# Seven-product steps: groups of products kept five places from their piece, copies first

## Chip, cores and metric

One core of a Trainium2 chip. The metric is the device time of one execution in microseconds; the program runs on one core, so its time is that core's.

## The reference, cut to what matters

```
X = rfft(x)                      # x: 2 x 3008 x 256
Y = shrink(X @ w + b)            # complex product, soft threshold
x = irfft(Y)                     # 6016 x 256
h = x @ w_in                     # first part, d_ff = 2048
x = (h * clip(h + 3, 0, 6) / 6) @ w_out
g = x @ w_gate                   # second part, d_ff = 1536
out = (silu(g) * (x @ w_val)) @ w_out2
```

All in float32. The kernel reaches float32 accuracy with three matmuls of a rounded type per product: each operand is split in a high half (a rounding copy, ScalarE) and a low half (the difference, VectorE).

## The kernel before, in words

The Fourier stage comes first, then the first part on the 6016 tokens, then the second. Tokens go in six pairs of two blocks, five pairs with 512 columns a block and a last one with 448. The first two pairs of the first part are computed plainly, unit by unit (`unit`, L552; its side work is in `beside`, L763). The other four pairs take **seven-product steps** (`quad1`, L875): a step has two blocks of tokens and two column groups of w_in, and gets their four products from seven (a Strassen scheme) instead of eight. The stage has 4 pairs x 8 steps = 32 steps. `quad` (L969) does the same for the second part in 72 steps.

A step of `quad1` runs so. `product` (L815) is three matmuls (L821 to L823). Products 1, 7 and 2 open the PSUM banks P, T and Q; ScalarE copies 1 and 7 out (`keep`, L868: c1, c7). VectorE adds c1 to Q (`add`, L863): v0, the first of four results. Product 6 is accumulated on P behind product 1 and copied (cu), 4 on T, whose sum with cu is g0; 5 on P, whose sum with c7 is g1; 3 on P again, which is the fourth result, read from P itself. Each result goes through `gate` (L855, ScalarE) and `times` (L859, VectorE) and then, by `give` (L845), through `split` (cast L517 on ScalarE, low half L130 on VectorE) into a *piece*. For each piece `give` puts two *groups* (three matmuls each, L125 to L127, into the accumulators of the output product) on the list `pending`. `fill` (L840) takes the first group from the list, if there is one; a step calls it at eight **places**. The multiply and split of the fourth result are left to the next step (`end_of`, L871), which does them ahead of its first product. A step so has 21 matmuls of products and 24 of groups.

The engines take their instructions in the order in which the program lists them, each engine for itself (the schedule is manual), and wait on semaphores between them. So an instruction that waits holds everything listed behind it on its engine.

`todo.send()` (L833) runs the next step of side work; it stands in four spots of a step. `beside1` (L932) says what it is: **operand steps** for the next pair (`operands`, L674: four differences and seven splits of the pair's tokens, `raw`, one instruction each, 18 in all) and **side steps** (`side`, L750), one step each of the chain that turns weights into the form of the seven products: for the second part, per block of weights, three word steps (VectorE and a scaling on ScalarE, L168 to L186), a step with the weight sums (L594, VectorE) and their cast into a ring slot (L632, ScalarE), a step with the low half, and one with the last low half and the store to memory (L639). The chain has twelve such blocks. What of it isn't done in the first part is done by two `side()` calls in each step of `quad`.

The ring has four slots of weights (`ring`, L589); `fetch` (L742) loads a step's weights two steps ahead on SP's queue, and the casts of the side chain take slots of the same ring. In steps 0 and 1 of a pair the tokens of the next pair come from the inverse transform (`post_raw`, L728: small matmuls L481 from a table `ct` that `load_ct`, L468, loads on SP's queue). At the end of a block, `finish1` (L507) copies an accumulator out and stores it on SP's queue. In `quad`, `share` (L976) runs the groups of the step before, and in the first step what is left on `pending`.

Of the kernel before, what the change touches and what calls it, by code (L numbers as in the profile page):

```python
# [83 lines left out]
def fourier_moe_kernel(ctx: ExitStack, tc: tile.TileContext, x, lin, bias, w1, w2, fwd1, inv2, fwd2,  # L84
# [342 lines left out]
    P = [lambda n=n: pre_conv(n) for n in range(NB * NT)]  # L427
# [246 lines left out]
    def operands(s, p, load=None):  # L674

        n = halves[p]
        todo = []

        def b(k, t):
            return raw[s][:, k, t * n : t * n + n]  # L680

        B[s] = {}
        T = {}

        def sub(i, x, y):
            T[i] = cv.tile([128, BLK], F32, tag="T", name=f"T{i}", bufs=3)
            nc.vector.tensor_tensor(out=T[i][:, :n], in0=x(), in1=y(), op=ALU.subtract)

        def hi(m, x):
# [12 lines left out]
        def r(k, j):  # L702
            return lambda: b(k, j)

        of = {1: r(0, 0), 7: t(3), 5: t(1), 6: t(2), 4: t(4), 2: r(1, 0), 3: r(1, 1)}
        subs = {5: (1, r(0, 1), r(0, 0)), 6: (2, r(1, 1), t(1)), 4: (4, r(1, 0), t(2)), 7: (3, r(1, 1), r(0, 1))}
        if load:
            todo += [load, lambda: None]
        for m, x in of.items():
            if m in subs:  # L710
                todo.append(lambda m=m: sub(*subs[m]))
            todo.append(lambda m=m, x=x: hi(m, x))
            todo.append(lambda m=m, x=x: lo(m, x))
        return todo

    def room_for(s):
        raw[s] = cv.tile([128, 2, 2 * BLK], F32, tag="raw", name=f"raw{s}", bufs=1)
# [45 lines left out]
    def beside(n):  # L763
        if not conv1.done():
            conv1.step()
        elif n < last - 1:
            side(1 + (n % 3 == 0))
        f = n - last
        if f in (0, 4, 8):
            load_ct(blocks[2 * S0 + f // 4])  # L770
        if f in (2, 3, 6, 7):
            if f == 2:
                begin_ops(f)
            post_raw(S0, f // 4, f % 4 - 2, bank)
        if f in (4, 5):
            next(ops)()
        if f >= 8:
            for _ in range(2 + f % 2):
                next(ops, lambda: None)()
        if f in (9, 13):  # L780
            fetch((f - 9) // 4)
# [28 lines left out]
    def acc_of(t, e):  # L810
        return (lambda shape, name: one_bank(spot[0], shape, name)) if t and e else acc_bank
# [25 lines left out]
    pending = []  # L837
    tail = []

    def fill(k=1):  # L840
        for _ in range(k):
            if pending:
                pending.pop(0)()

    def give(s, j, t, i, g):  # L845
        k, f = blocks[2 * s + t], 2 * j + i
        hi, lo = split(ghring(), glring(), g, halves[s])
        order = [(jj, ii) for jj in range(KF1 // 2) for ii in ((0, 1) if t == 0 else (1, 0))]
        at = order.index((j, i))
        for e in range(2):  # L850
            pending.append(lambda e=e: out1(k, f, e, hi, lo, at == 0, at == len(order) - 1, acc_of(t, e), "r"))

    def gate(x, n):
        r = xs_p.tile([128, BLK], F32, tag="r", name="r", bufs=3)
# [13 lines left out]
        nc.scalar.copy(c, x[:, :n])  # L868
        return c

    def end_of(q):  # L871
        if tail:
            tail.pop()()

    def quad1(q):  # L875


        s, j = quads1[q]
        n = halves[s]
        fetch(q + ASK)  # L880
        P, T, Q = bank_p(q), one_bank(spot[0] + 3, [128, BLK], "Tb"), bank_q([128, BLK], "Q")
        product = multiply(B[s], q, n)
        end_of(q)
        product(P, 1, start=True)
        c1 = keep(P, n)
        product(T, 7, start=True)
        c7 = keep(T, n)
        product(Q, 2, start=True)
        todo.send()
        v0 = add(Q, c1, n)  # L890
        r = gate(v0, n)
        fill()
        product(P, 6)
        cu = keep(P, n)
        fill()
        times(r, v0, n)
        product(T, 4)
        todo.send()
        g0 = add(T, cu, n)
        give(s, j, 0, 0, r)  # L900
        r = gate(g0, n)
        fill()
        if j < 2 and s + 1 < len(pairs):
            post_raw(s + 1, j, 0, bank_q)
        times(r, g0, n)
        fill()
        product(P, 5)
        g1 = add(P, c7, n)
        give(s, j, 0, 1, r)
        r = gate(g1, n)  # L910
        fill(2)
        if j < 2 and s + 1 < len(pairs):
            post_raw(s + 1, j, 1, bank_q)
            if j == 0:
                load_ct(blocks[2 * s + 3])
        todo.send()
        times(r, g1, n)
        fill()
        product(P, 3)
        give(s, j, 1, 1, r)  # L920
        fill()
        rv = gate(P, n)
        todo.send()
        slot.pop(q)

        def v1():
            times(rv, P, n)
            give(s, j, 1, 0, rv)

        tail.append(v1)  # L930

    def beside1(s):  # L932
        nxt = s + 1
        if nxt < len(pairs):
            o = operands(nxt, nxt)
            gap = 8
        else:
            o = operands(len(pairs), 0, from_dram(len(pairs), 0))
            gap = 2
        o = iter(o)  # L940
        for i in range(4 * (KF1 // 2)):
            if i < gap:
                if i % 3 != 1:
                    yield side
                else:
                    yield lambda: None
            elif i % 3 == 2:
                yield side
            else:
                def two(k=1 + (i % 2)):  # L950
                    for _ in range(k):
                        next(o, lambda: None)()
                yield two
        assert next(o, None) is None

    for q, (s, j) in enumerate(quads1):
        if q == 0:
            lower(units[-1])
            pending += outp(units[-2]) + outp(units[-1])
        if j == 0:  # L960
            todo.steps = beside1(s)
        quad1(q)
        if j == KF1 // 2 - 1 and s + 2 < len(pairs):
            load_ct(blocks[2 * s + 4])
# [4 lines left out]
    def quad(q):  # L969
# [5 lines left out]

        def share(t, e):  # L976
            if before is None:
                fill(2)
# [45 lines left out]
        end_of(q)  # L1024
        product(P, 1, start=True)
        c1 = keep(P, n)
        product(T, 7, start=True)
        c7 = keep(T, n)
        product(Q, 2, start=True)
        v0 = add(Q, c1, n)  # L1030
        if before is not None:
# [5 lines left out]
        side()  # L1037
        todo.send()
        share(0, 0)
        product(T, 4)  # L1040
# [11 lines left out]
        side()  # L1052
        todo.send()
        share(1, 0)

        last = q == len(quads2) - 1
# [59 lines left out]
```

## Time and profile before

| | us |
|---|---|
| median of 3 runs | 1284.1 (1282.96 to 1285.37) |
| the profiled execution | 1285.6 |
| its span, first to last instruction | 1283.8 |
| first seven-product step of the first part to the last | 345.5 to 734.5 |
| steps of the second part | from 734.5 |

The profile's busy shares of the span are PE 96%, DVE 70%, ACT 58%, POOL 1%; the granted clock of TensorE is 0.996 on average. In the profile PE is TensorE's matmuls, PEld its weight loads, DVE VectorE, ACT ScalarE, SP the engine that issues most DMAs; a q behind the name (SPq) is the engine's sequencer. A row of a timeline has the start, the duration, engine, line, operation, the tile written and those read, shapes, and in brackets the idle time of the engine just before it with what ended it. A row of stretches has its bounds, its length, the busy time (and instructions) of PE, PEld, DVE, ACT and POOL, the granted clock, and what the DMA engines did. Matmuls overlap: each lasts longer than the distance to the next.

### The profile page before, as it was taken

The numbers are of one execution on the slowest core, as the hardware profiler recorded it, in microseconds if no ns is written. First come the engines' busy times: TensorE is split into PE (matmuls) and PEld (weight loads), VectorE is DVE, ScalarE is ACT, GpSimd is POOL, SyncE is SP. The second block draws the span as 40 slices with busy tenths as digits, with TensorE's granted clock in tenths as the row PEclk, the third lists the DMA queues.
The fourth block names the chain that finished last, engine by engine and source line by source line (L and its number), as shares of the span: only waits on it lengthen the run. The fifth ranks groups of instructions, "written<-read, shape, count | busy, mean of one in ns | idle before, by whom it ended". The sixth has DMA issues, their size and how long they took to land.

```text
span 1283.8 us, 16138 instructions
## 1 busy us (share of the span) xinstructions
PE 1234.4 (96%) x5818; PEld 1006.0 (78%) x5818; DVE 902.3 (70%) x1606; ACT 742.6 (58%) x1348; POOL 11.1 (1%) x19
## 2 busy tenths in 40 slices
PE   8899999999999999999998999999999999999998
PEld 3699888888876686676776777788888888888897
DVE  3577686775677777777777778677677677666665
ACT  3355565555666666666666655666566556555554
POOL 3000000000000000000000000000000000000000
PEclk9999999999999999999999999999999999999999
DMA  7876222342334352261353366564454544644551
GB/s 283 314 230 196 82 75 100 127 151 73 145 117 148 123 201 101 103 216 71 140 188 120 139 216 227 185 222 174 176 191 170 206 166 161 233 148 151 214 183 68
DMA packets 54688, 209.62 MB, mean 163 GB/s; under 512 B 5376, under 2 KB 19040, under 8 KB 42976
## 3 DMA queue, kind: packets, MB, share of 16 engines
q1 hardware_dynamic: 47360, 199.43, 44.4%
q10 hardware_dynamic: 7056, 8.50, 1.8%
q8 instruction: 45, 0.74, 0.2%
q0 software_dynamic: 192, 0.66, 0.1%
q14 instruction: 35, 0.29, 0.1%
HBM read 162.17 MB, written 46.40 MB: 162 GB/s over the span
## 4 chain that ended last, share of the span: by engine, by line
PE 72%; DVE 13%; ACT 10%; issue 3%; DMA 2%; SPq 0%; ACTq 0%; DVEq 0%
PE acc L127 8%; PE acc L125 8%; PE acc L126 8%; PE P L821 6%; PE P L823 5%; PE P L822 5%; DVE r L859 4%; ACT gated L517 3%; ACT r L855 3%; PE Tb L823 3%; PE Tb L821 3%; PE Tb L822 3%; PE p L481 3%; PE ph L125 2%; PE ph L127 2%
## 5 line engine op out<-in xcount | busy, mean ns | idle before, releaser
L868 ACT COPY hold<-P 128x512 f32<-128x512 f32 (+1 forms) x208 | 119.1, 572 | 61.0 <-PE P L823 60.9
L130 DVE TENSOR_TENSOR gated<-s,gated 128x512 fp32r<-128x512 f32 (+1 forms) x144 | 97.4, 676 | 50.1 <-ACT gated L1003 49.4
L130 DVE TENSOR_TENSOR gated<-r,gated 128x512 fp32r<-128x512 f32 (+1 forms) x128 | 86.1, 673 | 54.3 <-ACT gated L517 51.7
L517 ACT CAST gated<-r 128x512 fp32r<-128x512 f32 (+1 forms) x128 | 77.6, 606 | 72.3 <-DVE r L859 72.3
L127 PE MATMUL acc<-gated,slot 128*128 128x512 f32 (+1 forms) x288 | 111.1, 386 | 0.0
L125 PE MATMUL acc<-gated,slot 128*128 128x512 f32 (+1 forms) x288 | 111.1, 386 | 0.0
L125 PE MATMUL acc<-gated,w_o 128*128 128x512 f32 (+1 forms) x256 | 102.4, 400 | 8.9 <-ACT gated L517 8.6
L126 PE MATMUL acc<-gated,slot 128*128 128x512 f32 (+1 forms) x288 | 111.0, 385 | 0.0
L127 PE MATMUL acc<-gated,w_o 128*128 128x512 f32 (+1 forms) x256 | 103.0, 402 | 4.8 <-DVE gated L130 4.7
L126 PE MATMUL acc<-gated,w_o 128*128 128x512 f32 (+1 forms) x256 | 98.4, 384 | 0.0
L863 DVE TENSOR_TENSOR hold<-Tb,hold 128x512 f32<-128x512 f32 (+1 forms) x104 | 70.3, 676 | 39.0 <-PE Tb L823 36.7
L1043 ACT ACTIVATE s<-hold 128x512 f32<-128x512 f32 (+1 forms) x72 | 44.8, 623 | 90.2 <-DVE hold L863 90.2
L855 ACT ACTIVATE r<-hold,three 128x512 f32<-128x512 f32 (+1 forms) x96 | 68.2, 710 | 49.6 <-DVE hold L863 42.4
L821 PE MATMUL P<-xo,slot 128*128 128x512 f32 x208 | 83.9, 403 | 11.7 <-ACT hold L868 10.7
L863 DVE TENSOR_TENSOR hold<-P,hold 128x512 f32<-128x512 f32 (+1 forms) x104 | 70.3, 676 | 34.9 <-PE P L823 34.7
L863 DVE TENSOR_TENSOR hold<-Q,hold 128x512 f32<-128x512 f32 (+1 forms) x104 | 70.3, 676 | 33.8 <-PE Q L823 25.0
L1003 ACT CAST gated<-s 128x512 fp32r<-128x512 f32 (+1 forms) x144 | 88.0, 611 | 10.2 <-DVE s L1060 8.9
L859 DVE SCALAR_TENSOR_TENSOR r<-r,hold 128x512 f32<-128x512 f32 (+1 forms) x96 | 64.7, 674 | 32.2 <-ACT r L855 31.3
L822 PE MATMUL P<-xo,slot 128*128 128x512 f32 x208 | 81.2, 390 | 0.0
L823 PE MATMUL P<-xo,slot 128*128 128x512 f32 x208 | 81.2, 390 | 0.0
L130 DVE TENSOR_TENSOR gs<-r,gs 128x512 fp32r<-128x512 f32 x64 | 44.1, 689 | 40.9 <-ACT gs L517 40.2
L127 PEld LDWEIGHTS acc<-gated,w_o 128*128 128x128 f32 x256 | 48.0, 187 | 29.9 <-DVE gated L130 22.2
(168 smaller groups left out, 3087.5 us busy)
## 6 DMA issues: line engine op xcount, KB each, us to landing
slot<-Wd SPq DMA_DIRECT2D x72, 1152.0 KB, 5.1
slot<-Sd SPq DMA_DIRECT2D x32, 896.0 KB, 5.1
st<-in_w SPq DMA_DIRECT2D x68, 256.0 KB, 4.2
Wd<-slot SPq DMA_DIRECT2D x12, 1152.0 KB, 5.1
Sd<-slot SPq DMA_DIRECT2D x8, 896.0 KB, 3.5
z<-Bd SPq DMA_DIRECT2D x12, 512.0 KB, 5.5
Cd<-cs ACTq DMA_DIRECT2D x12, 512.0 KB, 3.6
Xd<-x SPq DMA_DIRECT2D x20, 256.0 KB, 2.0
```

Of the source, the lines that this page charges most:

```text
L125: nc.tensor.matmul(o, wl, xh, start=start, stop=False)
L126: nc.tensor.matmul(o, wh, xh, start=False, stop=False)
L127: nc.tensor.matmul(o, wh, xl, start=False, stop=stop)
L130: nc.vector.tensor_tensor(out=o, in0=full, in1=hi.bitcast(F32), op=ALU.subtract)
L517: nc.scalar.copy(hi[:, :n], g[:, :n])
L821: nc.tensor.matmul(o, wl, x[m][:, 0, :n], start=start, stop=False, skip_group_check=not start)
L822: nc.tensor.matmul(o, wh, x[m][:, 1, :n], start=False, stop=False, skip_group_check=not start)
L823: nc.tensor.matmul(o, wh, x[m][:, 0, :n], start=False, stop=True, skip_group_check=not start)
L855: nc.scalar.activation(r[:, :n], x[:, :n], AF.Relu, bias=three)
L859: nc.vector.scalar_tensor_tensor(out=r[:, :n], in0=r[:, :n], scalar=6.0, in1=x[:, :n], op0=ALU.min, op1=ALU.mult)
L863: nc.vector.tensor_tensor(out=h, in0=x[:, :n], in1=c, op=ALU.add)
L868: nc.scalar.copy(c, x[:, :n])
```

## The change

`fill` takes a group only where at least five places have gone by since its piece was given; `drain` takes them without that rule, for the first step of the second part. In `quad1` and `quad` the copy of product 1 comes ahead of the old step's fourth result, whose multiply comes behind that copy and whose split behind the v0 add. The sends stand behind the copy of product 1, behind the copy of product 6 (ahead of the multiply of v0), behind the multiply of g0 and behind the multiply of g1. An operand step now has a copy on ScalarE and, on VectorE, a difference or the low half of an earlier copy: 11 steps. Side steps take three of the four sends in the first three steps of a pair and one send a step later: 14 for a pair, 56 in all, where there were 50 (13, 13, 13, 11). The second half of the inverse transform comes in step 2. In `quad` there is one send, and the two side steps stand together.

```
@@ -674,7 +674,6 @@
     def operands(s, p, load=None):
 
         n = halves[p]
-        todo = []
 
         def b(k, t):
             return raw[s][:, k, t * n : t * n + n]
@@ -704,14 +703,18 @@
 
         of = {1: r(0, 0), 7: t(3), 5: t(1), 6: t(2), 4: t(4), 2: r(1, 0), 3: r(1, 1)}
         subs = {5: (1, r(0, 1), r(0, 0)), 6: (2, r(1, 1), t(1)), 4: (4, r(1, 0), t(2)), 7: (3, r(1, 1), r(0, 1))}
-        if load:
-            todo += [load, lambda: None]
-        for m, x in of.items():
-            if m in subs:
-                todo.append(lambda m=m: sub(*subs[m]))
-            todo.append(lambda m=m, x=x: hi(m, x))
-            todo.append(lambda m=m, x=x: lo(m, x))
-        return todo
+        order = ((1, "sub", 7), (7, "lo", 1), (2, "sub", 5), (5, "lo", 7), (0, "sub", 6), (6, "lo", 2), (0, "sub", 4),
+                 (4, "lo", 6), (3, "lo", 5), (0, "lo", 4), (0, "lo", 3))
+
+        def step(h, what, m):
+            if h:
+                hi(h, of[h])
+            if what == "sub":
+                sub(*subs[m])
+            else:
+                lo(m, of[m])
+
+        return ([load] if load else []) + [lambda c=c: step(*c) for c in order]
 
     def room_for(s):
         raw[s] = cv.tile([128, 2, 2 * BLK], F32, tag="raw", name=f"raw{s}", bufs=1)
@@ -772,10 +775,8 @@
             if f == 2:
                 begin_ops(f)
             post_raw(S0, f // 4, f % 4 - 2, bank)
-        if f in (4, 5):
-            next(ops)()
         if f >= 8:
-            for _ in range(2 + f % 2):
+            for _ in range(2 - f % 2):
                 next(ops, lambda: None)()
         if f in (9, 13):
             fetch((f - 9) // 4)
@@ -837,10 +838,19 @@
     pending = []
     tail = []
 
+    LAG = 4
+    clock = [0]
+
     def fill(k=1):
         for _ in range(k):
+            clock[0] += 1
+            if pending and clock[0] - pending[0][0] > LAG:
+                pending.pop(0)[1]()
+
+    def drain(k):
+        for _ in range(k):
             if pending:
-                pending.pop(0)()
+                pending.pop(0)[1]()
 
     def give(s, j, t, i, g):
         k, f = blocks[2 * s + t], 2 * j + i
@@ -848,7 +858,7 @@
         order = [(jj, ii) for jj in range(KF1 // 2) for ii in ((0, 1) if t == 0 else (1, 0))]
         at = order.index((j, i))
         for e in range(2):
-            pending.append(lambda e=e: out1(k, f, e, hi, lo, at == 0, at == len(order) - 1, acc_of(t, e), "r"))
+            pending.append((clock[0], lambda e=e: out1(k, f, e, hi, lo, at == 0, at == len(order) - 1, acc_of(t, e), "r")))
 
     def gate(x, n):
         r = xs_p.tile([128, BLK], F32, tag="r", name="r", bufs=3)
@@ -868,9 +878,8 @@
         nc.scalar.copy(c, x[:, :n])
         return c
 
-    def end_of(q):
-        if tail:
-            tail.pop()()
+    def end_of():
+        return tail.pop()() if tail else lambda: None
 
     def quad1(q):
 
@@ -880,83 +889,78 @@
         fetch(q + ASK)
         P, T, Q = bank_p(q), one_bank(spot[0] + 3, [128, BLK], "Tb"), bank_q([128, BLK], "Q")
         product = multiply(B[s], q, n)
-        end_of(q)
         product(P, 1, start=True)
         c1 = keep(P, n)
+        end = end_of()
+        todo.send()
         product(T, 7, start=True)
         c7 = keep(T, n)
         product(Q, 2, start=True)
-        todo.send()
         v0 = add(Q, c1, n)
+        end()
         r = gate(v0, n)
         fill()
         product(P, 6)
         cu = keep(P, n)
+        todo.send()
+        times(r, v0, n)
         fill()
-        times(r, v0, n)
         product(T, 4)
-        todo.send()
         g0 = add(T, cu, n)
         give(s, j, 0, 0, r)
         r = gate(g0, n)
         fill()
-        if j < 2 and s + 1 < len(pairs):
-            post_raw(s + 1, j, 0, bank_q)
+        if j in (0, 2) and s + 1 < len(pairs):
+            post_raw(s + 1, j // 2, 0, bank_q)
         times(r, g0, n)
+        todo.send()
         fill()
         product(P, 5)
         g1 = add(P, c7, n)
         give(s, j, 0, 1, r)
         r = gate(g1, n)
         fill(2)
-        if j < 2 and s + 1 < len(pairs):
-            post_raw(s + 1, j, 1, bank_q)
+        if j in (0, 2) and s + 1 < len(pairs):
+            post_raw(s + 1, j // 2, 1, bank_q)
             if j == 0:
                 load_ct(blocks[2 * s + 3])
+        times(r, g1, n)
         todo.send()
-        times(r, g1, n)
         fill()
         product(P, 3)
         give(s, j, 1, 1, r)
+        rv = gate(P, n)
         fill()
-        rv = gate(P, n)
-        todo.send()
         slot.pop(q)
 
         def v1():
             times(rv, P, n)
-            give(s, j, 1, 0, rv)
+            return lambda: give(s, j, 1, 0, rv)
 
         tail.append(v1)
 
     def beside1(s):
-        nxt = s + 1
-        if nxt < len(pairs):
-            o = operands(nxt, nxt)
-            gap = 8
+        s += 1
+        if s < len(pairs):
+            o, do = iter(operands(s, s)), []
         else:
-            o = operands(len(pairs), 0, from_dram(len(pairs), 0))
-            gap = 2
-        o = iter(o)
+            o = iter(operands(s, 0, from_dram(s, 0)))
+            do = [next(o)]
         for i in range(4 * (KF1 // 2)):
-            if i < gap:
-                if i % 3 != 1:
-                    yield side
-                else:
-                    yield lambda: None
-            elif i % 3 == 2:
-                yield side
-            else:
-                def two(k=1 + (i % 2)):
-                    for _ in range(k):
-                        next(o, lambda: None)()
-                yield two
+            if i < 12:
+                do += [side] * (i % 4 != 3)
+            elif i % 2 == 0 or i == 31:
+                do.append(next(o))
+            elif i % 4 == 1:
+                do.append(side)
+            yield lambda: [g() for g in do]
+            do = []
         assert next(o, None) is None
 
     for q, (s, j) in enumerate(quads1):
         if q == 0:
             lower(units[-1])
-            pending += outp(units[-2]) + outp(units[-1])
+            pending += [(-LAG, g) for u in units[-2:] for g in outp(u)]
         if j == 0:
             todo.steps = beside1(s)
         quad1(q)
@@ -975,7 +979,7 @@
 
         def share(t, e):
             if before is None:
-                fill(2)
+                drain(2)
                 return
             (pb, fb), w, g = before
             if (pb, t, e) not in acc:
@@ -1021,20 +1025,20 @@
         fetch(F0 + q + ASK)
         P, T, Q = bank_p(F0 + q), one_bank(spot[0] + 3, [128, BLK], "Tb"), bank_q([128, BLK], "Q")
         product = multiply(B[len(pairs) + p], F0 + q, n)
-        end_of(q)
         product(P, 1, start=True)
         c1 = keep(P, n)
+        end = end_of()
         product(T, 7, start=True)
         c7 = keep(T, n)
         product(Q, 2, start=True)
         v0 = add(Q, c1, n)
+        end()
         if before is not None:
             (pb, fb), w, g = before
             hi = split_hi(g[1], pb)
             g[1] = (hi, split_lo(g[1], hi, pb))
         product(P, 6)
         cu = keep(P, n)
-        side()
         todo.send()
         share(0, 0)
         product(T, 4)
@@ -1049,8 +1053,7 @@
         nc.vector.tensor_tensor(out=s0[:, :n], in0=s0[:, :n], in1=v0, op=ALU.mult)
         hi = split_hi(s0, p)
         g0 = (hi, split_lo(s0, hi, p))
-        side()
-        todo.send()
+        side(2)
         share(1, 0)
 
         last = q == len(quads2) - 1
```

## Rows read from the trace of the kernel before

**Rows 1.** the page, part 4: the chain that ended last, shares by engine

```profile
PE 72%; DVE 13%; ACT 10%; issue 3%; DMA 2%; SPq 0%; ACTq 0%; DVEq 0%
```

**Rows 2.** three stretches: length, busy us by engine, TensorE clock, DMA share, GB/s

```profile
345.50:734.50 389.00, 362.44 (x1589) 278.86 (x1589) 292.92 (x526) 248.38 (x440) 0.00 (x0) 1.00 0.40 139
734.50:812.50 78.00, 70.97 (x299) 54.62 (x298) 60.05 (x114) 45.18 (x84) 0.00 (x0) 1.00 0.53 191
812.50:1200.00 387.50, 387.50 (x1713) 321.20 (x1712) 268.89 (x419) 230.49 (x402) 0.00 (x0) 1.00 0.52 187
```

**Rows 3.** timeline of PE: start, us, engine, line; first matmuls of second-part steps

```profile
744.07 0.40 PE L821 MATMUL P<-xo,slot 128*128 128x512 f32 x1
...
751.56 0.39 PE L821 MATMUL P<-xo,slot 128*128 128x512 f32 x1
...
1200.99 0.36 PE L821 MATMUL P<-xy,slot 128*128 128x448 f32 x1
...
1207.68 0.37 PE L821 MATMUL P<-xy,slot 128*128 128x448 f32 x1
```

**Rows 4.** timeline and line L481: inverse matmuls in the first-part stage, min/median/max ns

```profile
350.99 1.63 PE L481 MATMUL p<-inv_sb,ct 96*128 96x30 f32 x14
...
L481 PE MATMUL p<-inv_sb,ct x148: 191/275/328, 351.0 to 570.6; 96*128 96x94 f32 x104, 96*128 96x30 f32 x4, 96*128 96x12 f32 x4, 96*128 96x82 f32 x4
```

**Rows 5.** who waited for whom in 345.3 to 734.5: us, times, longest

```profile
PE P L821 <- ACT hold L868: 11.9, 20, 1.3
...
PE acc L125 <- ACT gated L517: 8.6, 23, 0.9
...
PE acc L127 <- DVE gated L130: 4.7, 11, 0.7
```

**Rows 6.** timelines of DVE, ACT and PE, steps 5 and 6 of the stage

```profile
410.32 0.68 DVE L859 SCALAR_TENSOR_TENSOR r<-r,P 128x512 f32<-128x512 f32 x1
...
411.03 0.62 ACT L517 CAST gated<-r 128x512 fp32r<-128x512 f32 x1 [1.95 <-DVE r L859]
...
411.56 0.58 ACT L868 COPY hold<-P 128x512 f32<-128x512 f32 x1
...
411.68 0.69 DVE L130 TENSOR_TENSOR gated<-r,gated 128x512 fp32r<-128x512 f32 x1 [0.69 <-ACT gated L517]
...
412.19 0.50 PE L821 MATMUL P<-xo,slot 128*128 128x512 f32 x1 [0.49 <-ACT hold L868]
...
412.29 0.28 DVE L173 TENSOR_SCALAR wt<-head 128x256 uint32<-128x256 uint32 x1
...
413.17 0.68 DVE L863 TENSOR_TENSOR hold<-Q,hold 128x512 f32<-128x512 f32 x1
...
413.88 0.72 ACT L855 ACTIVATE r<-hold,three 128x512 f32<-128x512 f32 x1 [0.92 <-DVE hold L863]
...
414.64 0.69 DVE L859 SCALAR_TENSOR_TENSOR r<-r,hold 128x512 f32<-128x512 f32 x1 [0.79 <-ACT r L855]
...
417.57 0.50 PE L127 MATMUL acc<-gated,w_o 128*128 128x512 f32 x1 [0.56 <-DVE gated L130]
...
425.05 0.69 DVE L130 TENSOR_TENSOR gs<-raw,gs 128x512 fp32r<-128x512 f32 x1
...
425.65 0.69 DVE L863 TENSOR_TENSOR hold<-Q,hold 128x512 f32<-128x512 f32 x1
```

**Rows 7.** waits in 734.5 to 812, and the timeline of PE

```profile
ACT slot L632 <- PE acc L127: 9.1, 3, 3.3
...
755.29 0.50 PE L821 MATMUL P<-xo,slot 128*128 128x512 f32 x1 [1.53 <-ACT hold L868]
```

**Rows 8.** timelines of SP's queue and of PE, steps 7 and 8

```profile
444.45 2.15 SPq L514 DMA_DIRECT2D Xd<-x  x2
...
446.65 0.42 SPq L474 DMA_DIRECT2D ct<-Cd  x1
...
451.64 1.70 PE L481 MATMUL p<-inv_sb,ct 96*128 96x40 f32 x14 [0.28 <-DMA ct<-Cd]
```

More of the change, by code (lines that the diff above doesn't have):

```diff
@@ L676, in operands @@
         n = halves[p]
-        todo = []
         def b(k, t):
@@ L706, in operands, with step @@
         subs = {5: (1, r(0, 1), r(0, 0)), 6: (2, r(1, 1), t(1)), 4: (4, r(1, 0), t(2)), 7: (3, r(1, 1), r(0, 1))}
[L707 to L714, printed above, removed]
+        order = ((1, "sub", 7), (7, "lo", 1), (2, "sub", 5), (5, "lo", 7), (0, "sub", 6), (6, "lo", 2), (0, "sub", 4),
+                 (4, "lo", 6), (3, "lo", 5), (0, "lo", 4), (0, "lo", 3))
+        def step(h, what, m):
+            if h:
+                hi(h, of[h])
+            if what == "sub":
+                sub(*subs[m])
+            else:
+                lo(m, of[m])
+        return ([load] if load else []) + [lambda c=c: step(*c) for c in order]
     def room_for(s):
@@ L774, in beside @@
             post_raw(S0, f // 4, f % 4 - 2, bank)
-        if f in (4, 5):
-            next(ops)()
         if f >= 8:
-            for _ in range(2 + f % 2):
+            for _ in range(2 - f % 2):
                 next(ops, lambda: None)()
@@ L838, in fourier_moe_kernel, with drain @@
     tail = []
+    LAG = 4
+    clock = [0]
     def fill(k=1):
         for _ in range(k):
+            clock[0] += 1
+            if pending and clock[0] - pending[0][0] > LAG:
+                pending.pop(0)[1]()
+    def drain(k):
+        for _ in range(k):
             if pending:
-                pending.pop(0)()
+                pending.pop(0)[1]()
     def give(s, j, t, i, g):
@@ L850, in give @@
         for e in range(2):
-            pending.append(lambda e=e: out1(k, f, e, hi, lo, at == 0, at == len(order) - 1, acc_of(t, e), "r"))
+            pending.append((clock[0], lambda e=e: out1(k, f, e, hi, lo, at == 0, at == len(order) - 1, acc_of(t, e), "r")))
     def gate(x, n):
@@ L869, in keep, with end_of @@
         return c
-    def end_of(q):
-        if tail:
-            tail.pop()()
+    def end_of():
+        return tail.pop()() if tail else lambda: None
     def quad1(q):
@@ L882, in quad1 @@
         product = multiply(B[s], q, n)
-        end_of(q)
         product(P, 1, start=True)
         c1 = keep(P, n)
+        end = end_of()
+        todo.send()
         product(T, 7, start=True)
@@ L888, in quad1 @@
         product(Q, 2, start=True)
-        todo.send()
         v0 = add(Q, c1, n)
+        end()
         r = gate(v0, n)
@@ L894, in quad1 @@
         cu = keep(P, n)
+        todo.send()
+        times(r, v0, n)
         fill()
-        times(r, v0, n)
         product(T, 4)
-        todo.send()
         g0 = add(T, cu, n)
@@ L902, in quad1 @@
         fill()
-        if j < 2 and s + 1 < len(pairs):
-            post_raw(s + 1, j, 0, bank_q)
+        if j in (0, 2) and s + 1 < len(pairs):
+            post_raw(s + 1, j // 2, 0, bank_q)
         times(r, g0, n)
+        todo.send()
         fill()
@@ L911, in quad1 @@
         fill(2)
-        if j < 2 and s + 1 < len(pairs):
-            post_raw(s + 1, j, 1, bank_q)
+        if j in (0, 2) and s + 1 < len(pairs):
+            post_raw(s + 1, j // 2, 1, bank_q)
             if j == 0:
                 load_ct(blocks[2 * s + 3])
+        times(r, g1, n)
         todo.send()
-        times(r, g1, n)
         fill()
@@ L920, in quad1 @@
         give(s, j, 1, 1, r)
+        rv = gate(P, n)
         fill()
-        rv = gate(P, n)
-        todo.send()
         slot.pop(q)
@@ L927, in v1 @@
             times(rv, P, n)
-            give(s, j, 1, 0, rv)
+            return lambda: give(s, j, 1, 0, rv)
         tail.append(v1)
     def beside1(s):
[L933 to L936, printed above, removed]
-        else:
-            o = operands(len(pairs), 0, from_dram(len(pairs), 0))
-            gap = 2
-        o = iter(o)
+        s += 1
+        if s < len(pairs):
+            o, do = iter(operands(s, s)), []
+        else:
+            o = iter(operands(s, 0, from_dram(s, 0)))
+            do = [next(o)]
         for i in range(4 * (KF1 // 2)):
[L942 to L953, printed above, removed]
+            if i < 12:
+                do += [side] * (i % 4 != 3)
+            elif i % 2 == 0 or i == 31:
+                do.append(next(o))
+            elif i % 4 == 1:
+                do.append(side)
+            yield lambda: [g() for g in do]
+            do = []
         assert next(o, None) is None
@@ L958, in fourier_moe_kernel @@
             lower(units[-1])
-            pending += outp(units[-2]) + outp(units[-1])
+            pending += [(-LAG, g) for u in units[-2:] for g in outp(u)]
         if j == 0:
@@ L977, in share @@
             if before is None:
-                fill(2)
+                drain(2)
                 return
@@ L1023, in quad @@
         product = multiply(B[len(pairs) + p], F0 + q, n)
-        end_of(q)
         product(P, 1, start=True)
         c1 = keep(P, n)
+        end = end_of()
         product(T, 7, start=True)
@@ L1030, in quad @@
         v0 = add(Q, c1, n)
+        end()
         if before is not None:
@@ L1036, in quad @@
         cu = keep(P, n)
-        side()
         todo.send()
@@ L1051, in quad @@
         g0 = (hi, split_lo(s0, hi, p))
-        side()
-        todo.send()
+        side(2)
         share(1, 0)
```

## The prediction

> **What bounds the kernel now.** I read the page's chain of waits first: nearly three quarters of the chain that ended last is TensorE, with VectorE and ScalarE in the rest [rows 1]. So TensorE is the resource, and the question is where it stands still. The busy view cut by stage answers that [rows 2]: from 812.5 us on TensorE is busy all the time, while in the stretch of the seven-product steps of the first part (345.5 to 734.5 us) and in the 78 us behind it idle time stands. That idle time undercounts, since a matmul's recorded 0.39 us holds its tail, which lies under the next matmul. The pace is better: a step of the second part that waits for nothing takes 33 matmuls from 744.07 to 751.56, so 0.227 us each at 512 columns, and from 1200.99 to 1207.68, so 0.203 us at 448 [rows 3]. The 32 first-part steps have 45 matmuls each, 24 steps at 512 columns and 8 at 448: 24 x 45 x 0.227 = 245.2 and 8 x 45 x 0.203 = 73.1. Between them stand 148 small inverse matmuls, 14 of which take 1.63 us: 17.2 [rows 4]. That is 335.5 of 389.0 us: **53.5 us are lost in this stage**. In the 78 us behind it nine steps at 7.49 would take 67.4: **10.6 us lost**.
>
> The waits of the stage name three losses [rows 5]: product 6 (P L821) waits for ScalarE's copy of product 1, and the groups of the output product wait for the high half (L125, from ScalarE) and the low half (L127, from VectorE) of a piece that was split shortly before.
>
> One step shows why [rows 6]. VectorE multiplies the old step's last piece at 410.32; ScalarE's cast of it waits for that until 411.03, and the copy of product 1 stands behind the cast, at 411.56, so product 6 starts at 412.19, over a microsecond after its turn. At 417.57 and later the groups wait for a piece only three places old. From one v0 add of VectorE to the next (413.17 to 425.65) it is 12.48 us, where TensorE needs 45 x 0.227 = 10.2. So the step is set by the hand-overs between ScalarE and VectorE, and TensorE's waits are where that shows. Moving groups alone would only shift the wait; the order on the two engines has to get shorter as well.
>
> **The change, part by part.**
>
> *Distance of five places.* Each step has eight places for a group. Now a piece given between places 2 and 3 is used at 5 and 6, one given before place 5 at 7 and 8. After: the pieces are used at 8 and 1', 2' and 3', 4' and 5', 6' and 7' (primes: next step). Five places are at least 5 x 3 x 0.227 = 3.4 us. A piece needs a multiply, a cast and a subtraction, 0.69 + 0.62 + 0.69 = 2.0 us by the rows' durations [rows 6], so 1.4 us of slack. The number of groups is unchanged; seven are left over for the first step of the second part, where four were, and its four shares take two each, so all fit. Cost: nothing, and the waits of L125 and L127 go. The rings of five split pieces are reused five pieces on; by the places above the last reader is at least two places ahead of that write. Cover exists.
>
> *Copies first.* Product 1's copy now stands ahead of the old piece's multiply and cast. Product 1 ends 0.68 + 0.16 = 0.85 us into the step, the copy takes 0.58 [rows 6], so it is done at about 1.45, and product 6 comes at 4 x 0.68 = 2.7. The wait goes, with 1.2 us to spare. What is queued behind the moved cast is the gate of v0 on ScalarE, whose result is needed by no matmul within 3.4 us.
>
> *What the order makes of VectorE.* I add it up by hand from v0 add to v0 add, for a full step with two operand steps and one side step of the word kind. Instructions back to back start 0.60 to 0.61 us apart (425.05 to 425.65) though each lasts 0.69; the word side step is 0.88 (412.29 to 413.17) [rows 6]. Now: 11 instructions of the step and 2 of operands, 13 x 0.605 = 7.9, plus 0.88, so 8.75. Waits that stay: the low half of the old piece for its cast 0.15; the low half of g0's predecessor for its cast 0.16; the multiply of g1 for its gate 0.26; the last low half for a whole cast 0.69 (as at 411.68, which waited 0.69). Sum 1.26, so 10.0, say **10.0 to 10.2, against 10.2 on TensorE**. Gone are the wait for a whole gate (0.79 at 414.64), the one for the old piece's cast (0.69 at 411.68), and a wait of an operand's subtraction for its own copy, which now comes one step later. So the two are level, and TensorE becomes the bound, just.
>
> Where it is not level: product 3 must follow the g1 add. By the same sum that add ends at 8.45 in the step and product 3 comes at 8.8, 0.35 us to spare; the third send now stands ahead of that add, so a long side step there (or a cast that waits for VectorE) makes TensorE wait. Full-width pairs: I put 1 us each, 3 us. The last pair is narrower: TensorE 45 x 0.203 = 9.1, VectorE loses only about 0.07 on 11 instructions and nothing on side steps and operands, so 9.3 to 9.6, 0.2 to 0.5 late in each of 8 steps, with 0.11 for each restart (a first matmul after a wait lasts 0.50 against 0.39 [rows 6, 3]): 4 us. Some slack of 1 us for what I do not see: **8 us left of 53.5**. Bounds: 1 us (all hidden) and 28 us (below).
>
> *Side work.* One weight block more (six side steps, of twelve blocks) moves from the second part into the first; it is inside the sum above. In the second part the cast of a block (L632) waited for its ring slot until the groups of the same step were done, 9.1 us in three times, and the copy of product 1 behind it held product 6 (1.53 us idle at 755.29) [rows 7]. Three such blocks cost most of the 10.6 us, some 2.5 each, and the first step about 2. After: two blocks, and both side steps stand at the later place, where the slot is nearly free. The cast then waits for the weight sums on VectorE instead and I still expect 1.4 to 2 us each: 3.6, the first step nothing. Bounds 0 and 7.6. **7 us saved.**
>
> *Inverse transform.* Inverse matmuls waited for their table (0.28 us idle at 451.64), whose load stood on SP's queue behind the two stores at 444.45 and was issued at 446.65 [rows 8]. Those stores now come in the next step, behind that load: the wait goes. Inside the 53.5. The second half of the inverse moves from step 1 to step 2, with its load a step earlier than needed; no cost. Operands start at step 3 instead of 2 and end at the last send; product 3, whose low half comes last, is the last product of the step. The operands in front of the stage: the same copies in the same steps, where TensorE waits for nothing; 0, bounds -1 and 1.
>
> **Sum.** 53.5 - 8 + 7 = 52.5. The profiled execution took 1285.6 (span 1283.8), the median of the runs shown is 1284.1, 1.5 lower. 1284.1 - 52.5 = 1231.6; I forecast **1231**. Bounds of the terms: 1284.1 - 52.5 - 7 - 3.6 = 1221 and, with 28 and 7.6 left, 1255.
>
> **Rivals.**
>
> *VectorE's chain stays longer.* If instructions there do not overlap in the new order, each of 13 costs 0.69 in place of 0.605: 1.1 more, 11.2 a step. Then product 3 waits 1.0 in 18 full steps without inverse and 1.2 in 8 narrow ones, with 26 restarts: 18 + 9.6 + 2.9 = 30, 22 over my 8: **1253**. For it: mutual waits of the two engines fill the step now. Against it: 425.05 to 425.65. The Trainium skill ("VectorE: DVE Perf Modes", Terms) speaks for this rival: a flush after every operation, and the next one cannot issue until the pipeline is empty. The trace does not agree, as the pair 0.60 apart at 0.69 length shows. Chance 0.20.
>
> *Slower.* Its place is the third send, between the multiply of g0 and the g1 add. If the chain stays at its 12.48 and six more side steps come on top (0.2 a step), then all of it lands on product 3: 2.5 in 18 steps, 45; in 8 narrow ones 2.5, 20; restarts 3; 68 against 60.5 saved: **1291**. It decides once the chain is over about 12.3 us a step. Against it: three of the waits in that chain have nothing left to wait for. Chance 0.04.
>
> *Nothing moves.* If copy and groups wait for other things that come no earlier, the waits keep their sum: **1284**, chance 0.04. Against: every wait in rows 5 has a releaser that is moved ahead.
>
> *All is hidden*: **1221**, within my forecast's own range.
>
> **Numbers.** Forecast 0.72 (own range 1221 to 1242), the rivals 0.20, 0.04, 0.04. The range 1220 to 1256 takes in the first two. 0.2%, 2.6 us, is about what a measurement tells from no change: faster 0.92, same 0.04, slower 0.04.
>
> **What would show it.** Right: the first-part stage is near 343 us and the 78 us behind it near 71; waits of product 6 for ScalarE's copy and of the groups for L517 and L130 nearly vanish; what stays is product 3 waiting for the g1 add, mostly in the last pair; the steps are 10.2 to 10.5 us apart. Wrong: steps at 11 us with product 3 or product 6 waiting in each, VectorE idle between its instructions for casts; or blocks of the second part still holding product 6 for 1.5 us.

## The result and the profile after

The changed kernel takes 1235.4 us (median of 4 runs, 1230.1 to 1236.6), the kernel before 1283.5 (4 runs): a ratio of 0.962, interval 0.9585 to 0.9649. The forecast was 1231, range 1220 to 1256.

In the page's chain of waits the share of TensorE has grown from 72% [rows 1]:

```profile
PE 82%; DVE 8%; ACT 5%; DMA 3%; issue 1%; SPq 0%; ACTq 0%; DVEq 0%
```

The busy view of the stretches that answer to [rows 2]:

```profile
347.40:692.70 345.30, 338.95 (x1581) 285.17 (x1580) 293.55 (x541) 248.09 (x443) 0.00 (x0) 1.00 0.47 166
692.70:773.00 80.30, 77.37 (x341) 63.43 (x340) 60.61 (x108) 49.19 (x88) 0.00 (x0) 1.00 0.52 190
```

In what follows **the stage** is the time from the first matmul of the first seven-product step to the first matmul of the second part, both read in the timeline of PE; **the ten steps** are those of the second part behind it. The stage went from 389.0 to 345.2 us, the ten steps from 85.5 to 80.3. VectorE and ScalarE are as busy in the stage as before (293.6 and 248.1 us), but it is 44 us shorter: the same work with fewer waits between them. What lies ahead of the stage (339.8 to 347.4 us over these kernels) varies with the execution, so lengths of stages compare kernels better here than whole times of single runs: the ten steps of the five kernels that have the same code there (the changed one and four below) agree within 0.1 us. In the table below, the time lost at a matmul is its distance to the one before it less the pace of [rows 3]; a product's loss is that of its three matmuls.

The waits of the stage that answer to [rows 5] (who waited for whom, us, times, longest):

```profile
PE P L822 <- ACT hold L878: 3.5, 1, 3.5
...
PE P L822 <- DVE hold L873: 1.6, 4, 0.7
...
PE Tb L822 <- ACT hold L878: 1.0, 1, 1.0
```

No wait of a group for a piece is left in that list. Product 6's 20 waits have become one. An undisturbed step (13) in the timeline of VectorE, from one v0 add to the next:

```profile
493.57 0.69 DVE L873 TENSOR_TENSOR hold<-Q,hold 128x512 f32<-128x512 f32 x1
494.18 0.68 DVE L130 TENSOR_TENSOR gated<-r,gated 128x512 fp32r<-128x512 f32 x1
...
495.66 0.69 DVE L869 SCALAR_TENSOR_TENSOR r<-r,hold 128x512 f32<-128x512 f32 x1
...
498.39 0.69 DVE L130 TENSOR_TENSOR xo<-raw,xo 128x512 fp32r<-128x512 f32 x1
498.99 0.68 DVE L873 TENSOR_TENSOR hold<-P,hold 128x512 f32<-128x512 f32 x1
...
500.52 0.69 DVE L869 SCALAR_TENSOR_TENSOR r<-r,hold 128x512 f32<-128x512 f32 x1 [0.25 <-ACT r L865]
501.96 0.69 DVE L130 TENSOR_TENSOR gated<-r,gated 128x512 fp32r<-128x512 f32 x1 [0.74 <-ACT gated L517]
...
503.77 0.69 DVE L873 TENSOR_TENSOR hold<-Q,hold 128x512 f32<-128x512 f32 x1
```

It is 10.20 us, where one was 12.48 [rows 6]. Two waits of the chain are left, 0.25 for the gate of g1 and 0.74 for a whole cast; the multiply of v0 (495.66) and the low half behind the v0 add (494.18) wait for nothing.

### The profile page after: what moved, and what is told of

Its sections match the earlier page's. It is cut to its first block, busy times and chain, and to the rows that moved or that the text cites. A ratio compares the mean times of both kernels' runs of the same rounds, so it can differ in the third digit from the quotient of the medians.

```text
span 1234.8 us, 16168 instructions
## 1 busy us (share of the span) xinstructions
PE 1210.8 (98%) x5818; PEld 1015.2 (82%) x5818; DVE 899.4 (73%) x1606; ACT 741.7 (60%) x1348; POOL 11.1 (1%) x19
## 4 chain that ended last, share of the span: by engine, by line
PE 82%; DVE 8%; ACT 5%; DMA 3%; issue 1%; SPq 0%; ACTq 0%; DVEq 0%
PE acc L125 10%; PE acc L127 10%; PE acc L126 10%; PE P L822 6%; PE P L824 6%; PE P L823 6%; PE Tb L822 3%; PE Tb L824 3%; PE Tb L823 3%; PE p L481 3%; PE ph L125 2%; PE ph L127 2%; PE ph L126 2%; DVE r L869 2%; PE p L285 2%; PE p L379 2%
## 5 line engine op out<-in xcount | busy, mean ns | idle before, releaser
L130 DVE TENSOR_TENSOR gated<-r,gated 128x512 fp32r<-128x512 f32 (+1 forms) x128 | 85.9, 671 | 29.7 <-ACT gated L517 26.8
L125 PE MATMUL acc<-gated,w_o 128*128 128x512 f32 (+1 forms) x256 | 99.6, 389 | 0.0
L126 PE MATMUL acc<-gated,w_o 128*128 128x512 f32 (+1 forms) x256 | 98.5, 385 | 0.0
L127 PE MATMUL acc<-gated,w_o 128*128 128x512 f32 (+1 forms) x256 | 98.4, 384 | 0.0
L1047 ACT ACTIVATE s<-hold 128x512 f32<-128x512 f32 (+1 forms) x72 | 44.9, 623 | 85.3 <-DVE hold L873 85.3
L1052 ACT ACTIVATE s<-hold 128x512 f32<-128x512 f32 (+1 forms) x72 | 45.0, 625 | 50.0 <-DVE hold L873 50.0
L130 DVE TENSOR_TENSOR gs<-r,gs 128x512 fp32r<-128x512 f32 x64 | 44.1, 689 | 40.1 <-ACT gs L517 39.4
```

What stands on the lines that cost most here:

```text
L125: nc.tensor.matmul(o, wl, xh, start=start, stop=False)
L126: nc.tensor.matmul(o, wh, xh, start=False, stop=False)
L127: nc.tensor.matmul(o, wh, xl, start=False, stop=stop)
L130: nc.vector.tensor_tensor(out=o, in0=full, in1=hi.bitcast(F32), op=ALU.subtract)
```

## Experiments

Where the stage lost time, at TensorE's pace, in us (the rest is small, except for 5.6 us at product 5 in the row with distance and copies):

| kernel | time | stage | ten steps | product 6 | groups | product 3 | product 4 |
|---|---|---|---|---|---|---|---|
| before | 1283.5 | 389.0 | 85.5 | 18.7 | 30.8 | 2.8 | 0.0 |
| distance only | 1279.8 | 388.0 | 85.9 | 39.4 | 3.5 | 10.9 | 0.7 |
| copies first only | 1254.8 | 364.0 | 84.2 | 0.5 | 23.5 | 2.8 | 0.0 |
| distance and copies | 1245.3 | 356.8 | 85.0 | 4.9 | 2.3 | 11.6 | 0.0 |
| changed, no distance | 1250.1 | 361.2 | 79.9 | 0.0 | 20.4 | 2.8 | 1.2 |
| changed, copies late | 1252.3 | 363.6 | 81.4 | 17.9 | 1.5 | 9.0 | 2.5 |
| **changed** | 1235.4 | 345.2 | 80.3 | 4.0 | 2.3 | 4.4 | 2.2 |

The first three rows below the kernel before add parts to it; the next two take one part out of the changed kernel. The times of these five are single runs, beside which the kernel before took 1282.1; the kernels below are single runs too, but for the last two. In each kernel with the distance three groups more, 1.8 us at TensorE's pace, go over from the stage to the ten steps, so such a kernel is compared with one without it by the sum of the two columns.

**Distance only.** `fill`, `drain` and `give` of the change in the kernel before.

```
+            if pending and clock[0] - pending[0][0] > LAG:
+                pending.pop(0)[1]()
```

> The kernel before with the distance of five places alone. My theory (the hand-overs between ScalarE and VectorE set the step, 12.5 us from v0 add to v0 add): the waits of the groups vanish but return as waits of product 6 and product 3, the stage of 389.0 us stays above 380, the time at 1275 to 1284. Rival (each wait removed is time gained): the groups' waits are about 30 us at TensorE's pace, so the stage falls to about 359 and the time to about 1255.

Measured: the stage at 388.0, the time at 1279.8; stage and ten steps together fell by 0.5 us. Its waits:

```profile
PE P L821 <- ACT hold L877: 32.1, 24, 2.3
...
PE P L821 <- DVE hold L872: 6.1, 11, 1.0
```

The groups' 30.8 us fell to 3.5, product 6 took 20.7 more and product 3 8.1. The rival falls: the wait was moved, almost all of it.

**Copies first only.** The head of the step as changed, in both parts, all else as before.

```
-        end_of(q)
         product(P, 1, start=True)
         c1 = keep(P, n)
+        end = end_of()
...
         v0 = add(Q, c1, n)
+        end()
```

> The kernel before with the copy of product 1 first and the old piece's cast behind the v0 add, nothing else. My theory: one wait of VectorE for a whole cast (0.69 us) leaves the chain of each of 26 steps without inverse, so the stage goes to 370 to 375 and the time to about 1268; product 6 no longer waits, the groups still do. Rival (each wait removed is time gained): product 6's 19 us, the stage 370 and the time 1265; the two differ in whether the groups' waits grow (theory) or keep their sum (rival).

Measured: the stage at 364.0, the time at 1254.8. It brings more than I or the rival said: product 6's 18 us, and the groups' loss, far from growing, fell by 7. The likely reason is that the shorter chain also brought the pieces earlier; no run shows that by itself.

**Distance and copies.** Both edits above; sends, operand steps and side work as before.

> The kernel before with the distance and the copies first, but sends, operand steps and side work as before. My theory: the chain still holds a wait for the gate of v0 (0.79) and for an operand's own copy (0.30), so 11.5 to 11.8 us a step, the stage at 365 to 372, the time at 1260 to 1268, the wait now at product 3. Rival (the waits of product 6 and of the groups were the loss, side work is along for the ride): the stage at 340 to 345, the time at about 1237.

Measured: 356.8 and 1245.3, most of the loss at product 3 (11.6). With copies first the distance is worth 6.5 us of stage and ten steps, alone 0.5. The stage came 8 us under my figure: steps 4 to 6 take the 11.5 us that I had, but steps 2 and 3, for example, run at TensorE's 10.2, and I had taken every step as a full one. The rival's 340 to 345 isn't reached either. The rest, 11.5 us of the stage, comes with the new sends, operand and side steps, and with them 4.7 of the ten steps; these were not tried one by one. At least 3.5 of the 11.5 has another cause than the chain: product 5 lost that in step 25, where ScalarE's cast of an operand waited 3.64 us for the load of the last pair's tokens, which the changed kernel sends at the start of step 24.

**No distance.** `LAG = 0` in the changed kernel.

> The changed kernel with a distance of one place instead of five. My theory: the chain is short, so only the pieces of g1, used two places after they are given, come late, by about 0.5 us in each of 26 steps: the stage goes from 345.2 to 355 to 360, the time to about 1248. Rival (the distance is what brought the gain): the groups' 30 us come back, the stage is at 370 or more, the time at 1260 or more.

Measured: 361.2, just above my range, and 1250.1. Its wait is the one expected, the groups for a low half:

```profile
PE acc L127 <- DVE gated L130: 11.5, 26, 1.3
```

26 times, as many as there are steps without inverse. With the short chain the distance is worth 15.5 us of stage and ten steps (16 of the stage).

**Copies late.** The changed kernel with `end = end_of(); end()` ahead of product 1.

> The changed kernel with the old piece's multiply and split ahead of product 1's copy again. My theory: the low half of the old piece waits for a whole cast again (0.5 to 0.7 us a step), product 1's copy comes about 1 us later; the stage goes from 345.2 to 357 to 362 us, the wait being mostly at product 6 and some at product 3. Rival (with the new sends and the distance the old order would be hidden too): the stage at 345 to 348.

Measured: 363.6 and 1252.3, product 6 waiting again:

```profile
PE P L822 <- ACT hold L878: 10.5, 23, 2.7
```

The place of the wait is my theory's, its size is not: 18.4 us where I had 12 to 17.

**What is left: the outputs' ring.** The largest single loss of the changed kernel is in step 25, which takes 14.7 us where TensorE needs 9.1. Timelines of SP's queue, ScalarE, VectorE and PE there:

```profile
611.41 0.56 SPq L727 DMA_DIRECT2D raw<-Xd  x1
613.25 0.33 SPq L639 DMA_DIRECT2D Wd<-slot  x1
...
615.69 2.44 SPq L514 DMA_DIRECT2D Xd<-x  x2
...
624.08 0.60 ACT L511 ACTIVATE x<-acc 128x512 f32<-128x512 f32 x1 [3.13 <-DMA Xd<-x]
...
624.71 0.69 DVE L513 TENSOR_SCALAR x<-acc 128x512 f32<-128x512 f32 x1 [3.10 <-DMA Xd<-x]
...
627.14 0.47 PE L822 MATMUL P<-gs,slot 128*128 128x448 f32 x1 [3.46 <-ACT hold L878]
...
629.23 0.57 PE L822 MATMUL Tb<-gs,slot 128*128 128x448 f32 x1
```

Four outputs of finished blocks fall into step 24 with the new distance, and they share a ring of three buffers with the gates. The row at 615.69 holds two stores: ScalarE waits for the first to land, VectorE for the second. Such stores land in 2.0 us in the median; these two took 8.3 and 6.8. They stand on the queue behind the load of a whole pair's tokens at 611.41 (1024 KB), which in this stage only the last pair has, and a store of weights at 613.25 (1152 KB); which of the two delays them was not tried. The loss has a second part (last section): the matmuls behind the wait last 0.57 us in place of 0.36.

Two kernels take the outputs out of the gates' ring, first into one ring of three (`s`, which the second part uses later), then into two, `s` and `T`. `T` is not wholly their own: it is the ring of the operand steps' differences, which come in other steps of a pair. The second:

```
+    xtag = ["s", "T"]
...
-            finish1(k, e, acc.pop((k, e)), xs_p, tag)
+            finish1(k, e, acc.pop((k, e)), xs_p if tag == "r" else cv, tag)
```

> The changed kernel with the outputs of finished blocks (the copy out of an accumulator, L507) in a ring of their own, three buffers that the second part uses later, instead of the ring of three that the gates use. My theory: the 3.5 us wait of step 25 (the first of the last pair but one; ScalarE and VectorE wait there for the landing of a store that still reads a buffer of the ring) and the spell at half clock behind it go, so the stage falls from 345.2 to 339 to 341 us. Rival (the step is late for its side work, three steps of it beside four finished blocks): the stage stays within 1 us of 345.2.

(Step 25 is the second step of the last pair.) Measured: the stage at 343.3, step 25 still at 13.2, time 1232.0. Of the four outputs the fourth now waited 2.9 us for the store of the first, as a ring of three must have it, so this kernel didn't tell the two theories apart. VectorE's row:

```profile
620.89 0.69 DVE L513 TENSOR_SCALAR x<-acc 128x512 f32<-128x512 f32 x1 [2.93 <-DMA Xd<-x]
```

> The changed kernel with the outputs of finished blocks in two rings of their own (three buffers for each of the two column halves), so that four of them in one step find four free buffers. With one ring of three the fourth still waited 2.9 us for the first one's store. My theory: step 25 takes 9.1 to 10 us instead of 14.7, the stage falls from 345.2 to 339.5 to 341. Rival (late for its side work): step 25 stays above 12 us.

Measured: the stage at 341.4, step 25 at 10.9, time 1230.0. The wait for the store is gone and with it 3.9 us of the stage; step 25 keeps a wait of 1.5 us of product 3 for VectorE, so about a third of what step 25 took beyond the pace was the rival's (14.7 to 10.9, with 9.1 as the pace). PE's row:

```profile
627.77 0.47 PE L822 MATMUL P<-gs,slot 128*128 128x448 f32 x1 [1.50 <-DVE hold L874]
```

**The first send behind product 7's copy.**

> The changed kernel with the first send behind the copy of product 7 instead of ahead of it. My theory: in steps 16 and 18 a cast into a ring slot waits on ScalarE for the weight sums and holds that copy, so product 4 is late (2.2 us with restarts); that goes, and the stage falls by about 2 us to 343. Rival (the cast then holds the gate of v0, and the same time comes back as a wait of product 3): the stage stays within 0.7 us of 345.2.

Measured: the stage at 344.6, time 1230.5. Steps 16 and 18 lost 1.7 us at product 4 and now lose nothing there (the other 0.5 of the table's 2.2 is in step 25 and stays); but step 25 got 0.7 longer, which hides it. Inconclusive by itself.

**All side work in the first part.** One more clause in `beside1`:

```
-            elif i % 4 == 1:
+            elif i % 4 == 1 or i % 4 == 3 and s < len(pairs):
```

> The changed kernel with all side work done in the first part: the fourth send of steps 3 to 6 of the first three pairs, which is empty, takes a side step (12 more). My theory: VectorE waits at that spot for a cast anyway, so the stage grows by less than 1 us, and the two waits of product 6 in the first steps of the second part (1.69 us each) go: the ten steps from 692.7 take 76.5 to 77 instead of 80.3, 3 us less in all. Rival (VectorE is full in the first part): the stage grows by 4 us or more, and nothing is won.

Measured: the stage at 354.2, the ten steps at 76.4, time 1241.7. The second half of my theory held, the first didn't. Timelines of ScalarE and PE at step 4:

```profile
393.83 0.94 ACT L632 CAST slot<-full 128x896 fp32r<-128x896 f32 x1 [1.69 <-DVE full L594]
...
395.78 0.57 ACT L878 COPY hold<-P 128x512 f32<-128x512 f32 x1
```

```profile
396.41 0.50 PE L822 MATMUL P<-xo,slot 128*128 128x512 f32 x1 [0.49 <-ACT hold L878]
```

The cast of a weight block stands on ScalarE and waits 1.69 us for the weight sums of its own side step on VectorE; the copy of product 1 is behind it. Six steps of the stage (4, 7, 12, 15, 20 and 23) take 1.5 to 1.9 us more than in the changed kernel, 10.3 us in all; the other steps take 1.3 less.

**The cast one side step later.** The sums alone in one step, the casts alone in the next, both low halves in the third.

```
                 weight_sums(F)
+                yield
                 t = ring()
                 nc.scalar.copy(t[:, :7], F[:, 1:])
-                yield
                 O = full.pop((f, 2))
                 nc.scalar.copy(t[:, 14:16], O)
-                low(t[:, 7:14], F[:, 1:], t[:, :7])
                 yield
+                low(t[:, 7:14], F[:, 1:], t[:, :7])
                 low(t[:, 16:], O, t[:, 14:16])
```

> The changed kernel with the cast of a weight block into its ring slot moved one side step on, so that no side step casts on ScalarE what VectorE makes in the same step; the low halves come together in the last step of a block. The amount of work is the same. My theory (ScalarE, in order, is held by a cast that waits for the weight sums): the waits of product 4 in steps 16 and 18 and of product 3 in step 1 go, 3 us, the stage falls from 345.2 to 341.5 to 343; the first steps of the second part stay as they are, since the sums and the cast stand together there. Rival (VectorE's amount of work makes TensorE late there): the stage stays within 0.7 us of 345.2.

Measured: the stage at 345.3, time 1230.7: a miss. Product 4's loss fell from 2.2 to 0.5 and step 1's went, but product 3's grew from 4.4 to 7.6. The wait that grew (1.6 us in 4 times in the changed kernel):

```profile
PE P L822 <- DVE hold L873: 4.2, 9, 1.1
```

With the changed kernel's sends the side work's place on VectorE, ahead of the g1 add, gives back what ScalarE gains: in step 9 the two low halves and a word step take VectorE 2.2 us ahead of that add, and product 3 waits 0.90 us.

**Two versions put together**, each with five runs beside the kernel before.

> The changed kernel with the outputs in two rings of their own and the first send behind the copy of product 7. Alone the first took the stage from 345.2 to 341.4, the second to 344.6. My theory (they mend different steps, 25 and 16 to 18): they add up, the stage at 340.5 to 341, the second part as it was, so 4 to 5 us under the changed kernel: a ratio to the kernel before of 0.957 to 0.960. Rival (the second only moves its wait): 341.4 again.

Measured: 1226.4 us, ratio 0.956 (0.954 to 0.9584), the stage at 339.0: more than the sum. Steps 16 and 18 keep what the later send won, and step 25, which that send alone had made 0.7 longer, now takes 10.3.

> The changed kernel with the outputs in two rings of their own, all side work in the first part, and the cast of a weight block a side step later. With all side work in the first part alone the stage grew by 9 us, in the steps behind a side step that casts what VectorE makes in the same step; the ten first steps of the second part fell from 80.3 to 76.4. My theory (the place of the casts cost the 9 us, not the amount of work): the stage at 341.5 to 344, the ten steps at 76.5, the ratio to the kernel before 0.954 to 0.957. Rival (the amount of VectorE's work): the stage at 348 or more, and no gain over the changed kernel's 425.5 for both together with the rings (421.6).

Measured: **1221.0 us**, ratio 0.951 (0.9489 to 0.953), clear of the changed kernel's 0.962 and better than I expected. The stage is 338.4 and the ten steps 76.4:

```profile
345.50:683.90 338.40, 335.58 (x1580) 284.34 (x1579) 301.93 (x567) 250.10 (x450) 0.00 (x0) 1.00 0.50 177
683.90:760.40 76.50, 76.50 (x342) 63.70 (x341) 52.48 (x82) 46.27 (x81) 0.00 (x0) 1.00 0.46 165
```

VectorE carries 8 us more work in the stage than in the changed kernel (301.9 against 293.6), and the stage is shorter by 6.8. So the amount of VectorE's work alone did not cost the 9 us. How much of the difference is the casts' place and how much the rings' (worth 3.9 us alone) was not tried apart, and why the later cast pays here but not by itself stays open.

## Why the prediction was right, step by step

**The loss and its cause.** Right. Stage and ten steps became 48.9 us shorter (43.7 and 5.2); the forecast was 52.5. From the first seven-product step to the end it is 50.9 in the two profiled executions, but 1.9 of that is no part of the change: issuing the last store took 2.07 us in that execution of the kernel before and 0.39 with the distance only, whose code is the same there. That moving groups alone only moves the wait is shown by the distance alone, 0.5 us; that the order on the two engines sets the step, by the copies, which alone win 26.3 us of stage and ten steps. What the forecast did not say is how much the parts need each other: the distance is worth 0.5, 6.5 or 15.5 us, by how short the chain already is.

**The chain by hand.** 10.0 to 10.2 forecast, 10.20 in step 13, with TensorE at 10.2 too. The waits summed to 1.26 by hand, and the row has 0.99 in two. That VectorE's instructions overlap is borne out in both traces: 493.57 to 494.18, 0.61 apart at 0.69 length. The rival of a chain at 11.2, and the slower one at 12.5, fall with that row: 16 of the 18 full-width steps without inverse are within 0.2 us of TensorE's pace.

**What is left: 8 us, in truth 11.5.** The sum's ideal of 335.5 must lose 1.8 (three groups that go over to the second part, 9 x 0.203), so 345.2 - 333.7 = 11.5. The products of the full-width pairs lost 3.5 (forecast 3), but only 1.8 of it at product 3, where the forecast had put it; 1.7 was lost in steps 16 and 18 at product 4, where the first send's cast held product 7's copy, so this term came out right partly by luck. The last pair's steps without step 25 lost 2.8 (forecast 4), and the inverses with what stands right behind them took 0.5 less than the 17.2 of the sum. The term that was mis-sized is "some slack of 1 us for what I do not see": step 25 alone lost 5.6, and 3.8 of that goes when the outputs leave a ring that the prediction never counted. The prediction went through the rings of the split pieces; it did not ask where the groups' last outputs go when four of them come in one step.

**The second part.** 7 us forecast. The ten steps fell by 5.2 although they carry the 1.8 us of three more groups: 7.0. The two blocks left cost 1.7 each, by the wait named. So product 6 is still held there for about 1.4 us, which the prediction's last paragraph lists as a sign of being wrong (1.5 us) though its sum had priced it: the sign was badly chosen. The rows of ScalarE and of PE at the first of them:

```profile
711.47 0.94 ACT L632 CAST slot<-full 128x896 fp32r<-128x896 f32 x1 [1.73 <-DVE full L594]
```

```profile
713.25 0.50 PE L822 MATMUL P<-xo,slot 128*128 128x512 f32 x1 [1.42 <-ACT hold L878]
```

The cast waits for the weight sums now, not for the slot as in [rows 7].

**The inverse.** Right: no matmul of the inverse waits for its table in the changed kernel.

## What to carry to other kernels

When TensorE's waits in a step are many and small, add up the chain of hand-overs between the engines that feed it, from one instruction to the same one a step later, with start-to-start distances: if that sum is above TensorE's own, a longer distance for the matmuls only moves the wait, and the order on those engines has to be mended first. A longer distance then pays, and it shifts everything that hangs on the last matmul of a group: count every ring that those late instructions share. Side work in which one engine waits for another within the same step holds the main work behind it; taking the two apart gained nothing by itself here, but stands in the fastest version.

## What the runs showed of the hardware beyond that

After TensorE had stood still for 3.46 us in step 25, its granted clock fell; the busy view of a stretch that holds most of the wait, and of the one behind it:

```profile
621.00:627.00 6.00, 2.67 (x14) 2.14 (x12) 2.14 (x4) 2.02 (x5) 0.00 (x0) 1.00 0.73 270
627.40:631.80 4.40, 4.40 (x15) 3.93 (x15) 3.99 (x12) 3.57 (x8) 0.00 (x0) 0.61 0.69 251
```

The matmuls of 448 columns last 0.57 us there, at the lower of the two clock levels (1.2 GHz), and are 0.37 us apart in place of 0.20, which adds about 1.4 us to the wait itself; the 0.61 is a mean that takes in the return to 2.4 GHz. In the stage of the kernel before, with waits of up to 1.3 us [rows 5], the granted clock is 1.00 [rows 2]. And the stores that landed late took 8.3 and 6.8 us where their kind takes 2.0: here a store of 256 KB, issued on the same queue within 5 us behind a load of 1024 KB and a store of 1152 KB, held its buffer for four times its usual time (8.3 us).
